# Sliding-window attention and a gated feed-forward layer on one core: the lead blocks' queries and keys loaded as fp32 by SyncE and ScalarE, and two lead blocks' scores also computed with the keys on the partitions

## The chip, the core and the metric

The kernel runs on one core of one Trainium2 chip. The metric is the device time of one execution in microseconds (us); less is better. A time is the median of several runs. A profile is one further execution, recorded by the hardware profiler.

## The reference

q, k and v are fp32 of 4 batches x 8 heads x 768 positions x 64. Each position attends to the first 4 positions (the sinks) and to the last 128 up to itself. The heads are put side by side, 3072 tokens of 512, and pass through a feed-forward layer with a hidden width of 2048. The output is fp32.

```python
scores = (1 / np.sqrt(D)) * np.matmul(q, k.transpose(0, 1, 3, 2))
keep = (pos[None, :] < n_sink) | ((rel >= 0) & (rel < window))   # 4 and 128
scores = np.where(keep, scores, -1e9)
a = np.exp(scores - scores.max(-1)); a = a / (a.sum(-1) + 1e-9)
x = (a @ v), heads side by side: (3072, 512)
h = x @ w_in; g = h / (1 + np.exp(-1.702 * h)); out = g @ w_out
```

## The kernel before, in words

**Tiling.** The 3072 tokens are 24 blocks of 128. A block's own keys and those of the block before it cover the window; the sinks are the batch's first 4 keys. Blocks 0, 6, 12 and 18 are the first of their batch. They have no block before them, and the 4 sinks are among their own keys. They run first (`ORD`) and are called the lead blocks here. Two blocks in the order of `ORD` make a group of 256 tokens for the feed-forward layer, so group 0 is blocks 0 and 6, group 1 is blocks 12 and 18, and there are 12 groups.

**A lead block's path.** Its queries and keys arrive as fp16 tiles `qkn` with tokens on the partitions. TensorE transposes them (`t_qk`, L408) into PSUM `tq`, and VectorE or ScalarE copies them to `qkT` (L282 to L288; the queries of a lead block are scaled on the way). TensorE first puts a mask into the PSUM tile `own` (`masks`, L455: identity times `bias0`) and adds the scores (`scores`, L463), queries on the partitions. VectorE takes each row's negated maximum (`mx`, L543). Half 0 of the heads goes through a subtraction on VectorE (`sub`, L600) and one exponential on ScalarE (L633). Half 1 is four exponentials on ScalarE with the maximum as bias (`exps`, L586). TensorE transposes the result so that keys are on the partitions (`t_a`, L696, PSUM `ta`), a copy makes `at`, TensorE multiplies by the values and a column of ones (`values`, L761, PSUM `av`), VectorE divides (`norm`, L776 and L777) into `xn`, TensorE transposes that (`t_x`, L790, PSUM `tx`), and a copy makes `xT`.

**The other 20 blocks** compute two score tiles (L488) and sink scores (L507), merge, take maxima and subtract on VectorE, take one exponential on ScalarE (L633), are transposed by DMA from SyncE's queue, and masked by two selections on GpSimd (L639, L645).

**The feed-forward layer.** `hT` (L825) is the first product; group 0 is split by block (16 matmuls of 128 columns per PSUM tile, tiles 0 to 3 for block 0 and 4 to 7 for block 6), the other groups use 8 matmuls of 256 columns. The gate is on ScalarE (L855), which loads a table whenever it changes between exponential and gate. `o` (L876) is the second product, 4 matmuls of 512 columns at a time. One tile `hT` and one such quarter of `o` both keep TensorE for about 0.87 us.

**Loads.** Only block 0's queries and keys come as fp32: `rawq` on SyncE's queue and `rawk` on ScalarE's (L237), each cast to fp16 on chip (L288). All other q, k, v and the weights are DMAs of GpSimd's queue, which cast on the way (L306, L315, L324, L333). Its order at the start is: q and k of 6, q and k of 18, k and q of 12, v of 0 and 18, q and k of 1, v of 6 and 12, three quarters of `w_in` (numbers 3, 1, 2), q and k of 2, `w_in` number 0.

**What sets the order.** The list `ORDER` names every operation by its number, with the engine that takes it, and each engine works through its own part of that list in order. An operation that waits holds up all that stand behind it on its engine. `FILL` puts matmuls on zeros (L905, into `misc`) ahead of given operations, 46 in all, every one of them before the first `hT`. `HOME` says for each PSUM tile which ring of banks it comes from.

Of the kernel before, what the change touches and what calls it, by code (L numbers as in the profile page):

```python
# [19 lines left out]
P = 128  # L20
D = 64
# [9 lines left out]
CFG = dict(  # L31
    tq=(0, 1, 2, 3, 4, 5, 6, 7),
# [10 lines left out]
    merge=4,  # L43
    pemask=(0, 1, 2, 3),
    f32=(0,),
# [8 lines left out]
RING = dict(qkn=4, qkt=4, e32=4, a16=4, at=4, atp=4, xn=2, xt=4, gt=3, osb=4, mm=3, own=2, pv=2, mi=1, th=2, ato=3, q0=4)  # L54
# [4 lines left out]
9V 4V 0S 17V 2V 15V 5G 13V 1S 22G 11V 19V 101S 18V 12V 7S 23G 6S 8S 28G 29G 20A 21A 3G 27G 108P 110P 109A 10V 113P  # L59
26G 16V 14V 130P 111V 114P 24G 32G 116V 131A 112A 132P 36G 133V 118A 115V 174P 37G 135P 117V 136P 175A 176P 138V  # L60
119A 154P 177V 25G 140A 120P 121A 137V 179P 31G 139V 180P 155A 152P 182V 35G 153V 141A 181V 33G 157P 184A 183V 142P
158P 34G 159V 122P 144P 185A 143A 40G 196P 123V 161V 126P 41G 145A 186P 160V 146P 198P 163A 148P 30G 127V 124P 187A
125V 46G 162A 188P 147V 164P 53G 149V 199A 166P 165V 150P 167V 189A 190P 168P 151V 128P 192P 169V 170P 129A 590P
171V 193V 582P 591A 197V 191V 172P 201P 47G 50G 586P 173A 194P 578P 583A 195V 587A 200P 579A 608P 49G 202V 610P 38G
55G 204V 203V 611A 609A 219P 221P 205V 588P 206V 589A 134A 580P 209V 208V 614P 39G 581A 105G 207V 222V 584P 42G 220V
576P 43G 585A 615A 612P 56G 577A 52G 613A 223P 604P 156A 225V 44G 226V 606P 45G 227V 616P 228V 224P 617A 607A 229V
232V 605A 230V 242P 618P 244P 231V 243V 592P 245V 626P 619A 210A 247P 246P 593P 249V 251V 248V 265P 267P 627P 250V
233A 620P 252V 266V 234S 254V 628P 268A 253V 621P 100S 255V 256A 211S 269P 622P 271V 257S 272V 594P 274V 288S 273V
629P 623P 624A 235G 270P 595P 630A 275V 104V 598P 596A 212G 599P 597S 276V 278V 631S 236P 277V 279A 238P 237V 600P
239V 59G 280S 213P 215P 51G 48G 214V 240P 601P 216V 241A 217P 602A 289P 61G 218V 290P 291V 642P 58G 292V 634P 71G  # L70
643A 294V 646P 293V 57G 295V 632P 68G 296V 647A 635A 297V 636P 62G 633A 306P 258G 640P 308V 309V 638P 641A 298V 310V
67G 73G 644P 311V 639A 637A 65G 648P 645A 654P 299A 64G 259P 655P 281G 307P 649P 312V 300S 313V 656P 314V 54G 261P
324S 315V 284P 260V 316A 650P 285V 262V 282P 657P 283V 301G 317S 178A 263P 286P 264V 651P 287V 603S 360S 664P 69G
652V 658A 662P 66G 665A 674P 60G 672P 70G 663A 675A 666P 78G 673A 325P 318G 660P 328V 327V 326P 304P 661A 667A 329V
668P 63G 330V 676P 669A 331V 74G 305V 670P 332V 302P 333V 671A 321P 303V 677P 322V 319P 682P 320V 334V 323S 342P
335A 344V 653S 345V 683P 678P 347V 343P 684P 346V 336S 348V 679P 350V 625S 351V 685P 349V 659S 352A 378P 692P 381V
686A 337G 353S 680V 379P 693A 696P 697A 380V 396S 690P 382V 80G 691A 383V 384V 688P 386V 76G 694P 385V 689A 102S
354G 387V 361P 695A 698P 364V 363V 700P 77G 699A 366V 340P 79G 701A 365V 338P 362P 388A 710P 339V 341V 355P 367V
711P 370V 368V 357P 356V 704P 389S 369V 702P 358V 371A 359S 414P 703A 705P 416V 372S 418V 712P 390G 417V 415P 706P
432S 419V 420V 713P 422V 83G 421V 707P 397P 82G 373G 708V 724P 400V 709S 399V 722P 423V 401V 714A 725A 393P 398P  # L80
402V 723A 391P 726P 392V 403V 394V 81G 716P 727A 85G 72G 718P 405V 404V 728P 719A 75G 374P 729A 717A 720P 86G 375V
106G 376P 721A 732P 406V 377V 424A 733P 395S 450P 738P 452V 407A 454V 451P 739P 453V 408S 730P 455V 456V 734P 457V
731A 715S 425S 458V 740P 433P 681S 746P 409G 436V 468S 435V 741P 747A 438V 735P 459V 742A 437V 92G 103S 758P 91G
434P 748P 759A 439V 426G 442V 736V 752P 749A 440V 756P 441V 753A 88G 744P 757A 95G 750P 745A 89G 412P 410P 413V 754P
107G 411V 429P 97G 755A 427P 430V 760P 751A 428V 443A 766P 431S 486P 767P 488V 460A 489V 444S 761P 490V 487P 762P
491V 461S 492V 768P 493V 743S 763P 494V 504S 445G 784P 764A 469P 785A 769P 472V 737S 462G 474V 495V 471V 782P 473V
772P 783A 470P 475V 87G 778P 773A 770V 98G 780P 446P 781A 84G 774P 447V 465P 775A 776P 466V 477V 779A 448P 777A 463P
476V 786P 464V 794P 449V 787A 478V 496A 467S 522P 788P 524V 525V 523P 789P 527V 479A 497S 795P 526V 528V 790P 530V
765S 529V 796P 480S 531V 532A 802P 94G 540S 498G 797P 803A 505P 798A 791P 507V 533S 96G 509V 800P 792A 481G 804P
499P 805A 810P 500V 90G 508V 814P 811A 510V 93G 501P 815A 506P 808P 511V 99G 801A 513V 484P 502V 812P 534G 482P 813A  # L90
806P 483V 809A 485V 822P 807A 514V 512V 503S 816P 515A 558P 687S 817P 793S 560V 559P 818P 562V 516S 823P 561V 563V
564V 819P 565V 567V 824P 566V 820V 568A 830P 517G 825P 831A 541P 834P 543V 826A 542P 535P 835A 827S 842P 536V 771S
544V 832P 569S 546V 833A 545V 821S 843A 547V 828P 799S 548V 836P 837A 550V 520P 829A 838P 521V 570G 549V 518P 839A
850P 551A 537P 538V 519V 844P 539S 851P 840P 552S 852P 841A 845P 573P 846P 574V 853P 553G 847P 854A 868P 855S 848A
856P 849S 869A 870P 857A 858P 871A 866P 862P 867A 859A 556P 554P 863A 557V 864P 571P 865A 860P 572V 555V 878P 861A
575S 872P 879P 873P 880P 874P 881P 886P 882V 875P 883S 887A 888P 876A 884P 877S 889A 894P 885A 890P 895A 896P 891A
892P 897A 898P 893A 906P 899A 900P 901P 907P 902P 912P 908P 903P 913P 904V 909P 914P 905S 910A 915P 911S 916A 917S
# [5 lines left out]
108:18 130:2 132:1 174:3 154:2 157:8 126:6 188:2 164:1 166:3  # L103
# [3 lines left out]
HOME = dict(x.split(":") for x in "0:pv 2:mm 5:own 7:own 8:mm 9:own 10:pv 12:pv 16:own 18:mm 19:pv 21:pv 22:mm 25:own 26:pv 27:mm 28:mm 29:pv 31:pv 32:own 35:pv 37:mm 40:own 41:pv 42:mm 43:mm 44:mm 46:mm 49:pv 50:pv 51:mm 52:own 53:own 54:own 55:pv 56:own 57:pv 59:mm 61:mm 62:own 63:own 64:own 65:pv 67:own 69:own 169:own 173:own 174:own 175:pv 180:pv 181:own 183:pv 185:own 189:pv 194:pv 197:pv 199:own 200:pv".split())  # L107
# [60 lines left out]
def kernel(  # L168
# [45 lines left out]
    bias0 = const.tile([P, P], BF16, name="bias0")  # L214
    bias1 = const.tile([P, 4], BF16, name="bias1")
# [16 lines left out]
    raw, o_raw = {}, {}  # L232
    for b in CFG["f32"]:
        for w, e in (("q", nc.sync), ("k", nc.scalar)):
            src = {"q": q, "k": k}[w][b // 6, :, b % 6 * P : b % 6 * P + P, :].rearrange("h s d -> s h d")
            raw[w, b] = const.tile([P, H, D], FP32, name=f"raw{w}{b}")
            o_raw[w, b] = hw(-3000, 0.4, lambda dst=raw[w, b], src=src, e=e: e.dma_start(dst, src), 0.7, late=1.15 if w == "q" else 0.3)  # L237
# [8 lines left out]
    )  # L246
    z_b = plan.add(DVE, -2002, 0.1, lambda: nc.vector.memset(bias0, 0.0))
# [18 lines left out]
    )  # L266
    z_k = plan.add(DVE, -90, 0.2, lambda: nc.vector.memset(ksb, 0.0))
# [12 lines left out]
    def copy(e, dst, src, factor=1.0):  # L280
        if e == DVE and factor != 1.0:
            nc.vector.tensor_scalar(out=dst, in0=src, scalar1=factor, scalar2=None, op0=ALU.mult)  # L282
        elif e == DVE:
            nc.vector.tensor_copy(out=dst, in_=src)  # L284
        elif factor != 1.0:
            nc.scalar.mul(out=dst, in_=src, mul=factor)
        else:
            nc.scalar.copy(out=dst, in_=src)  # L288
# [12 lines left out]
    def load_one(which, b, key, after, deps):  # L301
# [91 lines left out]
    for n, b in enumerate(ORD):  # L393
# [144 lines left out]
        mx = []  # L538
        for l in range(2):
# [6 lines left out]
                    deps=[packs[l]],  # L546
# [20 lines left out]
        subs = []  # L567
        a16 = Buf("a16", lambda n=n: a16s[n % RING["a16"]])
        bexp = []
        nbias, o_nb = small, top  # L570
        if nb and r > 0:
            nbias = const.tile([P, 2, 4], FP32, name=f"nb{b}")
            o_nb = plan.add(
                DVE, K0 - 38.75, 0.1,
                lambda nbias=nbias, small=small: nc.vector.tensor_scalar(
                    out=nbias, in0=small, scalar1=-scale, scalar2=None, op0=ALU.mult
                ),
                deps=[top, mx[0]],
            )
        factor = scale if r > 0 else 1.0  # L580
        for l in range(2):
            if l >= 2 - nb:

# [358 lines left out]
```

## Time and profile before

| | before |
|---|---|
| median of 3 runs | 227.57 us (227.36 to 228.15) |
| the profiled execution | 228.61 us |
| its span, first to last instruction | 226.9 us |
| mean granted TensorE clock | 1.000 |
| busy: TensorE, VectorE, ScalarE, GpSimd | 218.1, 138.7, 127.0, 115.3 us |
| first matmul of the feed-forward layer | 20.82 us |
| last eviction of an `o` tile starts | 223.76 us |
| matmuls of the feed-forward layer, L825 and L876 | 832 and 400 |

PE is TensorE's matmuls, PEld its weight loads, DVE VectorE, ACT ScalarE, POOL GpSimd, SP SyncE. A row of the time line gives the start and length of a run of like instructions, the engine, the line, the operation, the tiles written and read, and, in brackets, the idle time ahead of it with what ended it. The table of stretches gives for each stretch the busy time of each engine with the number of instructions, then the granted clock, the mean load of the DMA engines and what they moved in GB/s. A transfer that casts is counted with the bytes it writes.

### The profile page before, as it was taken

Reading aid. Unit: us, or ns where it says so; the run is one execution under the profiler, and the core shown is the slowest. Engines: PE = TensorE matmul, PEld = TensorE weight load, DVE = VectorE, ACT = ScalarE, POOL = GpSimd, SP = SyncE. Lnnn points to the kernel's source line nnn. Section 1 sums busy time; section 2 is a strip of 40 time slices with the busy share of each in tenths; the row PEclk is TensorE's granted clock in tenths of the full one; section 3 lists DMA queues with packets and bytes.
Section 4 is the critical chain, followed back from the end, with each engine's and each line's share of the span. In section 5 each row is a group of like instructions: output and inputs, shape, how many; then the busy total and the mean of one; then the engine's idle time right before and its main releaser. Section 6 shows DMA issues by size and latency. Waiting matters only on the chain.

```text
span 226.9 us, 5434 instructions
## 1 busy us (share of the span) xinstructions
PE 218.1 (96%) x2238; PEld 153.7 (68%) x2238; DVE 138.7 (61%) x332; ACT 127.0 (56%) x197; POOL 115.3 (51%) x127
## 2 busy tenths in 40 slices
PE   7889999999998999999999999999999999999994
PEld 4668997445774875775685685695695685775862
DVE  5799648876948288888976666668467582031001
ACT  3788675543663744767259347456656666540721
POOL 8995583029996970671980891570790321300000
PEclk9999999999999999999999999999999999999999
DMA  9999999999999999899997999998998175202202
GB/s 127 155 166 205 181 179 200 181 178 236 145 104 148 191 152 165 217 158 125 176 164 107 243 101 121 195 136 101 219 136 181 27 237 97 97 0 49 92 0 92
DMA packets 131992, 32.82 MB, mean 145 GB/s; under 512 B 124640, under 2 KB 129024, under 8 KB 131968
## 3 DMA queue, kind: packets, MB, share of 16 engines
q0 software_dynamic: 77024, 13.37, 78.1%
q1 hardware_dynamic: 53904, 18.85, 40.9%
q10 hardware_dynamic: 1040, 0.26, 0.5%
q8 instruction: 17, 0.28, 0.5%
q14 instruction: 7, 0.06, 0.1%
HBM read 27.36 MB, written 6.29 MB: 148 GB/s over the span
## 4 chain that ended last, share of the span: by engine, by line
PE 85%; DVE 7%; POOL 3%; ACT 2%; issue 1%; POOLq 0%; DVEq 0%
PE hT L825 35%; PE o L876 35%; PE own L488 3%; PE av L761 2%; PE av L765 2%; PE prv L488 2%; PE av L755 2%; DVE mx L562 2%; DVE mx L543 1%; POOL qkn L315 1%; PE tq L408 1%; DVE e L600 1%; POOL at L639 1%; ACT a L586 1%; PE tx L790 1%
## 5 line engine op out<-in xcount | busy, mean ns | idle before, releaser
L825 PE MATMUL hT<-xT,w_in 128*128 128x256 f16 (+1 forms) x832 | 91.9, 264 | 0.3 <-DVE osb L284 0.3
L876 PE MATMUL o<-w_out,gT 128*128 128x512 f16 (+1 forms) x400 | 90.5, 371 | 0.0
L855 ACT ACTIVATE gT<-hT 128x512 f16<-128x512 f32 x96 | 54.9, 597 | 49.9 <-PE hT L825 49.1
L825 PEld LDWEIGHTS <-w_in 128*128 128x128 f16 x832 | 74.0, 98 | 11.9 <-issue 0.7
L876 PEld LDWEIGHTS <-gT 128*128 128x128 f16 x400 | 36.5, 98 | 34.2 <-DVE own L531 0.4
L645 POOL TENSOR_SCALAR_AFFINE_SELECT atp<-at 128x1024 f16<-128x1024 f16 x20 | 22.1, 1104 | 71.2 <-DMA at<-a 54.7
L531 DVE COPY_PREDICATED own<-later,prv 128x512 f32<-128x512 uint16 x40 | 26.7, 692 | 25.4 <-PE prv L488 24.1
L633 ACT ACTIVATE a<-e 128x1056 f16<-128x1056 f32 (+1 forms) x24 | 23.8, 1007 | 18.2 <-issue 8.8
L543 DVE TENSOR_REDUCE mx<-own 128x4 f32<-128x512 f32 x48 | 31.9, 686 | 1.2 <-PE own L463 0.5
L600 DVE TENSOR_TENSOR e<-own,mx 128x512 f32<-128x512 f32 x44 | 28.9, 683 | 1.0
L639 POOL TENSOR_SCALAR_AFFINE_SELECT at<-at 128x1024 f16<-128x1024 f16 x20 | 22.3, 1113 | 1.4
L776 DVE RECIPROCAL rcp<-av 128x4 f32<-128x4 f32 x48 | 8.5, 176 | 23.4 <-PE av L765 23.2
L315 POOL DMA_DIRECT2D qkn<-in_k_dram x23 | 20.9, 911 | 2.8 <-DMA w_in<-in_moe_w_in_dram 2.4
L306 POOL DMA_DIRECT2D v<-in_v_dram x24 | 21.5, 907 | 0.8 <-DMA w_out<-in_moe_w_out_dram 0.8
L315 POOL DMA_DIRECT2D qkn<-in_q_dram x23 | 21.0, 913 | 1.8 <-DMA w_in<-in_moe_w_in_dram 1.7
L777 DVE TENSOR_TENSOR xn<-av,rcp 128x256 f16<-128x256 f32 x48 | 20.4, 424 | 1.7
L288 ACT COPY osb<-o 128x512 f32<-128x512 f32 (+1 forms) x17 | 9.2, 561 | 19.3 <-PE o L876 13.2
L761 PE MATMUL av<-v,at 128*128 128x65 f16 x192 | 16.7, 194 | 0.5 <-POOL at L639 0.4
L284 DVE COPY osb<-o 128x512 f32<-128x512 f32 x8 | 5.5, 688 | 18.5 <-PE o L876 18.1
L761 PEld LDWEIGHTS <-at 128*128 128x128 f16 x192 | 14.0, 98 | 3.1 <-POOL at L639 1.3
L765 PE MATMUL av<-v,atp 128*128 128x65 f16 x160 | 14.9, 194 | 0.0
L488 PEld LDWEIGHTS <-qkT 64*128 64x128 f16 x320 | 9.4, 94 | 7.0 <-issue 5.7
(59 smaller groups left out, 176.9 us busy)
## 6 DMA issues: line engine op xcount, KB each, us to landing
out_dram<-osb SPq DMA_DIRECT2D x23, 256.0 KB, 2.6
v<-in_v_dram POOLq DMA_DIRECT2D x24, 128.0 KB, 5.4
qkn<-in_q_dram POOLq DMA_DIRECT2D x23, 128.0 KB, 5.1
qkn<-in_k_dram POOLq DMA_DIRECT2D x23, 128.0 KB, 5.1
w_in<-in_moe_w_in_dram POOLq DMA_DIRECT2D x4, 512.0 KB, 10.1
w_out<-in_moe_w_out_dram POOLq DMA_DIRECT2D x4, 512.0 KB, 10.2
at<-a SPq DMA_TRANSPOSE x20, 3.5
rawk<-in_k_dram ACTq DMA_DIRECT2D x1, 256.0 KB, 4.5
```

The costliest lines, as they stand in the source:

```text
L306: return sw(key, 0.88, lambda: nc.gpsimd.dma_start(v65[:, b, :, 0:D], src), 1.0, deps=[z_1] + deps, after=after)
L315: key, 0.88, lambda: nc.gpsimd.dma_start(buf()[:, i, w], src), 0.9,
L531: nc.vector.copy_predicated(out=own[l](), mask=later.unsqueeze(1).to_broadcast((P, 4, P)), data=prv[l]())
L543: lambda l=l, own=own, small=small, r=r: nc.vector.tensor_reduce(out=small[:, l], in_=own[l](), axis=AX.X, op=ALU.max, negate=r == 0),
L600: nc.vector.tensor_tensor(out=e32()[:, 512 * l : 512 * l + 512].rearrange("p (j s) -> p j s", j=4), in0=own[l](), in1=small[:, l].unsqueez ...
L633: nc.scalar.activation(out=a16()[:, lo:hi], in_=e32()[:, lo:hi], func=AF.Exp, scale=factor)
L639: nc.gpsimd.affine_select(out=dst()[:, lo : lo + n], in_=at()[:, lo : lo + n], pattern=[[0, n], [1, P]], compare_op=ALU.is_ge, fill=0.0, b ...
L645: nc.gpsimd.affine_select(out=dst()[:, lo : lo + n], in_=at()[:, lo : lo + n], pattern=[[0, n], [-1, P]], compare_op=ALU.is_gt, fill=0.0, ...
L761: nc.tensor.matmul(av()[:, j], ato()[:, c], v65[:, b, h], start=(r == 0), stop=(r == 0))
L825: nc.tensor.matmul(ht()[:, n], w_in16[:, c, bass.ts(f, P)], xt[g]()[:, tok, c], start=(c == 0), stop=(c == 3))
L855: lambda fs=fs, cols=cols, gt=gt, ht=ht: nc.scalar.activation(out=gt()[:, fs[0] : fs[-1] + 1, cols], in_=ht(), func=AF.Gelu_apprx_sigmoid),
L876: nc.tensor.matmul(po(), gt()[:, F, bass.ts(t, P)], w_out16[:, F, cols], start=(F == 0), stop=(F == NF - 1))
```

## The change

1. **Loads.** Queries and keys of all four lead blocks come as fp32, four on SyncE's queue and four on ScalarE's, and are cast on chip, the cast now also possible on GpSimd. By the new order the casts are on ScalarE (q of 0, 6, 12), VectorE (k of 6, q of 18) and GpSimd (k of 0, 12, 18). ScalarE issues three loads ahead of its first table load and the fourth behind its first cast. GpSimd's queue of transfers then begins with v of 0 and 6, `w_in` 3, v of 12, `w_in` 0 and 1, v of 18, `w_in` 2, and q and k of 1; the casts stand between them.
2. **Scores with keys on partitions** for blocks 0 and 6 (`direct`). The scores are still computed with queries on the partitions and their maxima taken, but only for the maxima. VectorE splits the negated maximum into two bf16 parts (`nm`), TensorE transposes them (`tm`), a copy makes `nmt`. Two PSUM tiles `st` collect a transposed mask, the scores with operands exchanged and, through the 0/1 matrix `pick`, the maxima; two exponentials of 128 x 512 write `at` at once. The subtraction, the five exponentials, the transposes `t_a` and their copies are not made for these two blocks.
3. **Order.** `ORDER`, `FILL` (20 matmuls instead of 46) and `HOME` are new throughout. Ahead of the first `hT` there no longer stand: the transposes of block 1, the `t_a` of block 18, and the products `av` of blocks 12 and 18.

```diff
-    f32=(0,),
+    direct=(0, 1),
+    f32=(0, 6, 12, 18),
...
+            raw[w, b] = (
+                sb("osb", (P, d_model), FP32, f"raw{w}{b}") if n >= 2 else Buf("raw", lambda w=w, b=b: raws[w, b])
+            )
...
             return plan.add(
-                {DVE: 0.45, ACT: 0.6}, -95 + w, 0, lambda e: copy(e, buf()[:, i, w], raw[which, b]),
-                deps=[o_raw[which, b]], take=[buf],
+                {DVE: 0.45, ACT: 0.62, POOL: 0.75}, -95 + w, 0, 
+                lambda e: copy(e, buf()[:, i, w], raw[which, b]().rearrange("p (h d) -> p h d", h=H)),
+                deps=[o_raw[which, b]], take=[buf], give=[raw[which, b]],
             )
...
+            def shift(nm=nm, small=small):
+                nc.vector.tensor_copy(out=nm[:, 0], in_=small)
+                nc.vector.tensor_tensor(out=nm[:, 1], in0=small, in1=nm[:, 0], op=ALU.subtract)
...
+                lambda tpm=tpm, nm=nm: nc.tensor.transpose(tpm(), nm.rearrange("p a l j -> p (a l j)"), identb),
...
+            def masks_t(st=st):
+                for l in range(2):
+                    nc.tensor.matmul(
+                        st[l](), identb, bias0t.unsqueeze(1).to_broadcast((P, 4, P)), start=True, stop=False
+                    )
+            def scores_t(st=st, b=b):
...
+                        nc.tensor.matmul(
+                            st[l]()[:, j], qk_of(b)[rows, 4 + j], qk_of(b)[rows, j], start=False, stop=False
+                        )
...
+                def shift_t(l=l, st=st, nmt=nmt):
+                    for j in range(4):
+                        h = 4 * l + j
+                        nc.tensor.matmul(
+                            st[l]()[:, j], pick[:, h : h + 1].to_broadcast((16, P)), nmt, start=False, stop=j == 3
+                        )
...
+                        lambda l=l, st=st, at=at: nc.scalar.activation(
+                            out=at()[:, 4 * l : 4 * l + 4], in_=st[l](), func=AF.Exp
+                        ),
```

The three lists of the order are left out of this cut.

More of the change, by code (lines that the diff above doesn't have):

```diff
@@ L266 @@
     )
+    o_pick = None
+    if CFG["direct"]:
+        o_pick = plan.add(
+            DVE, -2000, 0.1,
+            lambda: nc.vector.tensor_tensor(out=pick, in0=identb[0:16, 0:8], in1=identb[0:16, 8:16], op=ALU.add),
+            deps=[o_identb],
+        )
     z_k = plan.add(DVE, -90, 0.2, lambda: nc.vector.memset(ksb, 0.0))
@@ L683 @@
+                subs.append(
+                    plan.add(
+                        DVE, K0 - 38.7, 0.6, sub, deps=[top if r > 0 else None, mx[l]], take=[e32], give=[own[l]]
+                    )
                 )
-            e_snk = None
             if r > 0:
-                e_snk = plan.add(
-                    ACT, K0 - 36, 0.15, lambda a16=a16, e32=e32, f=exp: f(a16, e32, 1024, 1056),
-                    deps=[subs[-1]] + zero, take=[a16], give=[e32], table="exp",
-                )
```

419 lines of the change are left out of this document (236 added, 183 removed).

## The prediction

> **What bounds the kernel now.** First the page's table of busy time, then the groups of instructions:
>
> ```profile
> PE 218.1 (96%) x2238; PEld 153.7 (68%) x2238; DVE 138.7 (61%) x332; ACT 127.0 (56%) x197; POOL 115.3 (51%) x127
> L825 PE MATMUL hT<-xT,w_in 128*128 128x256 f16 (+1 forms) x832 | 91.9, 264 | 0.3 <-DVE osb L284 0.3
> L876 PE MATMUL o<-w_out,gT 128*128 128x512 f16 (+1 forms) x400 | 90.5, 371 | 0.0
> ```
>
> TensorE is the bound, and the idle time ahead of its two big groups is 0.3 us in all. So from the first `hT` on, time is the work. What could be won lies before it. The time line of the start, and then of the end:
>
> ```profile
> 0.81 0.46 SPq L237 DMA_DIRECT2D rawq<-in_q_dram  x1
> 4.58 0.62 ACT L288 CAST qkn<-rawq 128x512 f16<-128x512 f32 x1 [1.98 <-DMA rawq<-in_q_dram]
> 5.30 0.62 ACT L288 CAST qkn<-rawk 128x512 f16<-128x512 f32 x1
> 7.04 0.42 DVE L284 COPY qkT<-tq 128x512 f16<-128x512 f16 x1 [1.16 <-ACT qkT L286]
> 7.52 0.40 PE L463 MATMUL own<-qkT 64*128 64x128 f16 x8 [0.27 <-DVE qkT L284]
> 7.96 0.69 DVE L543 TENSOR_REDUCE mx<-own 128x4 f32<-128x512 f32 x1 [0.49 <-PE own L463]
> ...
> 20.35 0.41 DVE L284 COPY xT<-tx 128x512 f16<-128x512 f16 x1
> 20.82 1.39 PE L825 MATMUL hT<-xT,w_in 128*128 128x128 f16 x22
> ...
> 223.76 0.37 ACT L288 COPY osb<-o 128x256 f32<-128x256 f32 x1 [0.46 <-PE o L876]
> ```
>
> The first `hT` starts at 20.82, once VectorE has copied the `xT` of block 6 at 20.35. VectorE works from 7.04 to there nearly without a break: the table of stretches gives it 12.63 us busy in the 14.32 from 6.50. So VectorE's queue sets the start. 46 of TensorE's matmuls there are fill and only look like work. The rest is an account in two parts: **T0**, the start of the first `hT`, and what TensorE does from T0 to 223.76, which is 202.94 us before. The end, 3.14 us of span behind 223.76, is built alike in both kernels and stays.
>
> **Part 1: T0 in the changed kernel.** I follow VectorE's new queue from the first item that waits for a load, the cast of k of block 6.
>
> Arrival of k6. `rawq` and `rawk` were issued at 0.81 and landed 3.7 and 4.5 us later. Now q6 and k6 stand right behind them in the same two queues. What the DMA engines moved while the two were under way:
>
> ```profile
> 2.00:2.50 0.50, 0.50 (x4) 0.38 (x3) 0.30 (x4) 0.50 (x1) 0.50 (x2) 1.00 0.89 205
> 2.50:3.00 0.50, 0.50 (x4) 0.34 (x3) 0.12 (x3) 0.10 (x1) 0.50 (x1) 1.00 0.73 167
> 3.00:3.50 0.50, 0.50 (x5) 0.35 (x3) 0.50 (x1) 0.00 (x0) 0.50 (x2) 1.00 1.27 287
> 3.50:4.00 0.50, 0.50 (x4) 0.38 (x3) 0.50 (x1) 0.00 (x0) 0.50 (x1) 1.00 1.35 280
> ```
>
> (The last column is GB/s.) Two pieces of 262 KB are 0.52 MB. Bounds for the next pair: 1.85 us at 284 GB/s, 3.1 us at 167. I take the faster, since two loads were moving in that row and a queue of loads is now behind them: k6 at 4.65 (mean of the two landings) + 1.85 = **6.5 us**.
>
> From there VectorE has, in order, by rows of before: cast of k6 0.45 (no row; bounds 0.20, the 128x128 cast L265, and 0.69, the fp32 128x512 subtraction; near the 0.42 of the 128x512 copy); queries of block 0 to `qkT` 0.42; wait for `own` 0.50 (7.46 to 7.96 above); two `mx` 1.37; the two `nm` operations 0.5 (0.19 as L615 and 0.34 as L562, both small); two copies to `ksb` 0.4 (0.197 each); `pick` 0.2; two `mx` of block 6 1.37; `nm` 0.5; cast of q18 0.45; copy `nmt` 0.2 (bounds 0.11, the smallest memset, and 0.42); two `mx` of block 12 1.37; subtraction 0.69; four `norm` 2.18 (0.545 from one to the next); `qkT` of block 18 0.42; three memsets 0.33; `xT` 0.41. That is 11.8. Before it was 8 `mx` 5.5, 4 subtractions 2.8, `qkT` 1.7, `at` 1.2, norms 2.2, `xT` 0.4 = 13.8. For handovers I add 0.5, about a third of the 1.7 that VectorE idled in that stretch before: **T0 = 6.5 + 11.8 + 0.5 = 18.8 us**, 2.0 earlier.
>
> What lies beside it. ScalarE: casts 3 x 0.62, four copies of 0.6, `nmt` 0.3, four exponentials 2.5 (0.63 each, L633, in place of the 1.14 + 0.63 per block), copy, then the exponentials of block 12 end near 18.2 and `xT` of block 0 near 19.4, while TensorE needs it for its second tile at 18.8 + 0.89 = 19.7. GpSimd's casts have no row; bounds 0.55 (half the 1.11 of the 128x1024 selection) and 1.17 (the 32x520 product L363). Cast of k0 from 5.3 to 6.1 stays ahead of VectorE's 6.5 to 7.4, so it is covered; uncovered, it would cost its excess one for one. The new work on TensorE per direct block, masks 0.43, scores 0.23, `tm` 0.06, maxima 8 x 0.055, against 0.44 for the `t_a`, fits where the 46 fills stood: nothing.
>
> Weights. GpSimd's queue issues `w_in` 3 behind the cast of k12, near 10; before at 12.28, landing 7.5 to 12.8 later. Its way is clearer: the first 12 transfers of that queue moved at 155 GB/s until 15, ahead of `w_in`; now two v do. At the 205 GB/s of the weights (2.55 us a piece) I estimate landings near 14.5, 18, 20.5 and 24 for numbers 3, 0, 1, 2. They are needed at 18.8, 19.7, 22.4 and 25.5: hidden by 1.5 us or more; with T0 below 17 they would be the next wait.
>
> **Part 2: from T0 to the end.** 202.94 stays, and what stood ahead of the first `hT` moves behind it: transposes of block 1 and `t_a` of 18, 16 x 0.055 = 0.88; `av` of 12 and 18, 16 x 0.03 = 0.48. Sum 204.3. Waits: the stall at 54.56, 0.38 us for GpSimd's selection of block 1, goes, since between the scores of block 1 and its `av` the new order gives 21 us and the gate tiles ahead of its exponential end as early as before. Other visible stalls (0.4 to 0.8 us each near 62, 70, 131 and 185) are redealt by the new order; zero on balance, bounds -2 and +2 (there were about 2.5 to lose). One new wait is in the open: the exponentials of block 18 stand ahead of the load of the gate's table, and the first gate then starts near 23.3, before at 22.62; by then four `hT` wait in PSUM. I cost it at nothing, since TensorE's fifth tile comes at 23.2 and the banks of block 18's transposes are free by then; uncovered 0.7.
>
> Sum: 18.8 + 204.3 - 0.4 = 222.7 against 223.76, **-1.1 us** of the profiled 228.61 (span 226.9). That run lies 1.04 above the median, so I take the difference: 227.57 - 1.1 = 226.5, own range 225.5 to 227.4 from the cast's bounds, handovers 0 to 1.2, and half of the redealt stalls. About 0.3% (0.7 us) can be told from no change.
>
> **The rivals.**
>
> *B, the loads come late; slower.* All waits on k6. At 167 GB/s two pairs need 6.3 us from 2.0, and the row of `rawk` has 0.7 between its last bytes and its cast: k6 at 9.0, T0 = 21.3, end 21.3 + 204.3 - 0.4 = 225.2, time 229.0. It decides for slower from a k6 at 8.3 on. For it: eight such pieces now stand where two stood. Against: 287 GB/s. The Trainium skill, "DMA: Bandwidth & Descriptors", section "Issuing engines are not separate DMA queues", says that loads issued from SyncE, ScalarE and GpSimd run on the same 16 DMA engines and that spreading them saves only issue time. The load column above 1 where both kinds ran agrees that they share. By that rule alone no pair would gain a rate, which is this rival.
>
> *C, the head start is eaten.* `hT` begins at 18.8 but TensorE waits: 0.7 for the first gate, and 0.4 to 0.8 in stalls of the new order (scores of blocks 3 and 4 come some 2.5 us later than before, their `av` 2.5 sooner). 226.5 + 1.1 = 227.6. For it: the table load ended at 22.62 before and cannot come earlier now.
>
> *D, more is won.* Casts at their lower bounds, k6 at 6.0, T0 18.0, and the new order loses 1.5 of the 2.5 stalls: 226.5 - 0.8 - 1.5 = 224.2.
>
> *E, TensorE goes slow in the gaps.* The first 18 fills took 4.02 us, 0.22 each, where 0.11 is the later rate; 26 of the fills are gone. If TensorE fell back to that rate before T0, the first 4 us of `hT` would take 2 more: 228.5. Against: no gap of TensorE's from 5.5 to 20.8 is longer than 0.91 us, and in the queues above I see none over 1. The Trainium skill, "TensorE: Matmul & The Clock Gate", section "What's actually happening", puts the fall at an idle window of about 3.4 us. By that rule E does not occur; the trace has no such gap to show it.
>
> That the change doesn't do what it says would need the loads to stay on GpSimd; the new queues show them moved.
>
> **Chances.** Forecast 0.48, B 0.13, C 0.20, D 0.14, E 0.05. Faster: 0.42 of the forecast, D, and 0.03 of C, 0.59. Within 0.3%: 0.06 of the forecast, 0.14 of C, 0.02 of B, 0.22. Slower: 0.11 of B, E, 0.03 of C, 0.19. Range 224.5 to 228.4: it holds the forecast, C, most of D and the near half of B and E.
>
> **What would show it.** VectorE's cast of k6 starting near 6.5; the first `hT` near 18.8, right behind VectorE's copy of `xT`; no wait of TensorE for `w_in`; first gate near 23.3; no gap at the selection of block 1. Wrong if k6 is cast after 8, if the first `hT` waits for `w_in` or ScalarE, or if TensorE's idle time behind T0 grows by over 1 us.

## The result, and the profile after

The changed kernel takes **231.07 us** (229.74 to 232.43, 4 runs) against 227.49 (227.36 to 228.15, 4 runs): ratio 1.0143, 95% interval 1.0100 to 1.0187. It is slower by 3.6 us; I had forecast 226.5, with 228.4 as the upper end. Its profiled execution took 231.13 us (span 229.4, granted clock 0.997). In the runs below, one execution each of e2, e6 and e8 (235.9, 234.9 and 235.2 us) fell into a slower state and is left out of their medians.

The page's busy time and two groups of instructions of the changed kernel:

```profile
PE 219.3 (96%) x2234; PEld 152.7 (67%) x2234; DVE 140.0 (61%) x344; ACT 125.4 (55%) x186; POOL 111.1 (48%) x124
...
L922 PE MATMUL hT<-xT,w_in 128*128 128x256 f16 (+1 forms) x832 | 93.3, 264 | 0.2 <-DMA xT<-xn 0.2
...
L858 PE MATMUL av<-v,at 128*128 128x65 f16 x192 | 16.8, 194 | 2.5 <-POOL at L736 2.5
```

And from the full lists of groups, the fills, changed and before; then before's wait of `av` (total, times, longest):

```profile
L1002 PE MATMUL misc<-fill 128*128 128x256 f16 x20 | 5.1, 383 | 1.1 <-DVE fill L286 1.1
...
L905 PE MATMUL misc<-fill 128*128 128x256 f16 x46 | 8.6, 330 | 1.1 <-DVE fill L261 1.1
...
PE av L761 <- POOL at L639: 0.4, 1, 0.4
```

TensorE is still the bound. The fills take 5.1 us instead of 8.6, yet TensorE is busy 1.2 us longer, and `av` waits 2.5 us for GpSimd's selections where it waited 0.4. The time line, from the cast of k6 to the last eviction:

```profile
7.88 0.72 DVE L317 CAST qkn<-rawk 128x512 f16<-128x512 f32 x1 [2.47 <-DMA rawk<-in_k_dram]
...
9.84 0.69 DVE L579 TENSOR_REDUCE mx<-own 128x4 f32<-128x512 f32 x1 [0.77 <-PE own L499]
...
11.18 0.82 DVE L616 CAST nm<-mx 128x8 bf16<-128x8 f32 x1
...
13.38 1.29 DVE L579 TENSOR_REDUCE mx<-own 128x4 f32<-128x512 f32 x2 [0.59 <-PE own L499]
...
21.03 0.42 DVE L317 COPY xT<-tx 128x512 f16<-128x512 f16 x1
...
21.60 1.95 PE L922 MATMUL hT<-xT,w_in 128*128 128x128 f16 x32
...
226.17 0.37 ACT L323 COPY osb<-o 128x256 f32<-128x256 f32 x1 [0.50 <-PE o L973]
```

k6 comes 1.4 us later than forecast, VectorE waits for `own`, and the first `hT` starts at 21.60 instead of 18.8, even behind the 20.82 of before.

**Where the time went.** No fill stands behind 30 us in any of the kernels. So TensorE's end is 30 plus the work left there plus its idle time behind it. One row of the table of stretches holds both (length of the stretch, then PE's busy time). For the changed kernel, to its last matmul:

```profile
30.00:226.14 196.14, 193.16 (x1919) 133.88 (x1916) 120.02 (x288) 106.02 (x147) 91.62 (x95) 1.00 1.15 141
```

And for a second profile of the kernel before (run e17 below, 227.53 us, at its median):

```profile
30.00:222.64 192.64, 191.39 (x1890) 132.22 (x1887) 114.78 (x272) 105.26 (x149) 92.40 (x95) 1.00 1.14 142
```

Work left: 193.16 against 191.39, 1.77 more. Idle: 196.14 - 193.16 = 2.98 against 1.25, 1.73 more. Together 3.5, the whole loss. One half was lost before 30 us, the other in waits behind it.

### The profile page after: what moved, and what is told of

Same layout as the page of the kernel before. It is cut to its first block, busy times and chain, and to the rows that moved or that the text cites. A ratio compares the mean times of both kernels' runs of the same rounds, so it can differ in the third digit from the quotient of the medians.

```text
span 229.4 us, 5445 instructions
## 1 busy us (share of the span) xinstructions
PE 219.3 (96%) x2234; PEld 152.7 (67%) x2234; DVE 140.0 (61%) x344; ACT 125.4 (55%) x186; POOL 111.1 (48%) x124
## 4 chain that ended last, share of the span: by engine, by line
PE 65%; DMA 15%; POOL 8%; issue 4%; ACT 3%; DVE 2%; SPq 0%; ACTq 0%; POOLq 0%
PE o L973 27%; PE hT L922 25%; DMA w_out<-in_moe_w_out_dram 5%; DMA qkT<-qkn 5%; DMA rawk<-in_k_dram 3%; POOL qkn L351 3%; POOL atp L742 2%; POOL at L736 2%; DMA xT<-xn 2%; PE av L858 2%; PE own L524 2%; PE av L862 2%; PE av L852 1%; PE prv L524 1%; PE tq L444 1%
## 5 line engine op out<-in xcount | busy, mean ns | idle before, releaser
L922 PE MATMUL hT<-xT,w_in 128*128 128x256 f16 (+1 forms) x832 | 93.3, 264 | 0.2 <-DMA xT<-xn 0.2
L730 ACT ACTIVATE a<-e 128x1056 f16<-128x1056 f32 (+1 forms) x22 | 22.7, 1041 | 12.1 <-issue 9.2
L699 DVE TENSOR_TENSOR e<-own,mx 128x512 f32<-128x512 f32 x42 | 27.8, 682 | 1.3 <-ACT gT L952 0.5
L323 ACT COPY osb<-o 128x512 f32<-128x512 f32 (+1 forms) x15 | 8.3, 554 | 23.4 <-PE o L973 20.2
L351 POOL DMA_DIRECT2D qkn<-in_q_dram x20 | 18.0, 901 | 5.6 <-DMA w_out<-in_moe_w_out_dram 4.6
L351 POOL DMA_DIRECT2D qkn<-in_k_dram x20 | 17.8, 895 | 2.9 <-DMA w_in<-in_moe_w_in_dram 2.4
L858 PE MATMUL av<-v,at 128*128 128x65 f16 x192 | 16.8, 194 | 2.5 <-POOL at L736 2.5
L317 DVE COPY osb<-o 128x512 f32<-128x512 f32 x10 | 6.9, 686 | 11.1 <-PE o L973 10.5
```

What stands on the lines that cost most here:

```text
L351: key, 0.88, lambda: nc.gpsimd.dma_start(buf()[:, i, w], src), 0.9,
L699: nc.vector.tensor_tensor(out=e32()[:, 512 * l : 512 * l + 512].rearrange("p (j s) -> p j s", j=4), in0=own[l](), in1=small[:, l].unsqueez ...
L730: nc.scalar.activation(out=a16()[:, lo:hi], in_=e32()[:, lo:hi], func=AF.Exp, scale=factor)
L858: nc.tensor.matmul(av()[:, j], ato()[:, c], v65[:, b, h], start=(r == 0), stop=(r == 0))
L922: nc.tensor.matmul(ht()[:, n], w_in16[:, c, bass.ts(f, P)], xt[g]()[:, tok, c], start=(c == 0), stop=(c == 3))
```

## The experiments

Theory after the result: (1) the start is late since 20 fills leave TensorE at about half its rate there and k6 lands late; (2) behind it a second bound, the way from GpSimd's loads by SyncE's DMA transposes to GpSimd's selections and `av`, takes what the start wins. Rival: the start alone; whatever it wins arrives at the end.

All medians in us; the kernel before beside them was at 227.5 to 227.9. Ratios to it with 95% intervals. "hT" is the start of the first `hT`, "left" and "idle" as above, all three from the one profiled run, which took the time given.

| run | median | ratio | profiled | hT | left | idle |
|---|---|---|---|---|---|---|
| before, first profile | 227.57 | | 228.61 | 20.82 | 191.81 | 1.92 |
| e17 before, second profile | 227.86 | 0.9992 [0.9955, 1.0028] | 227.53 | 20.78 | 191.39 | 1.25 |
| changed | 231.07 | 1.0143 [1.0100, 1.0187] | 231.13 | 21.60 | 193.16 | 2.98 |
| e1 changed, 35 fills | 229.20 | 1.0066 [1.0041, 1.0091] | 230.49 | 21.26 | 192.90 | 2.61 |
| e2 changed, one queue | 231.77 | 1.0208 [1.0151, 1.0264] | 231.56 | 22.83 | 194.30 | 2.23 |
| e3 before, 32 fills | 228.00 | 1.0014 [0.9980, 1.0048] | 228.17 | 21.89 | 192.36 | 0.93 |
| e4 changed, old loads | 232.15 | 1.0215 [1.0163, 1.0267] | 232.04 | 20.50 | 192.27 | 4.93 |
| e12 old loads, 35 fills | 229.96 | 1.0099 [1.0061, 1.0138] | 230.64 | 19.61 | 191.71 | 4.05 |
| e7 before + loads | 234.06 | 1.0281 [1.0252, 1.0309] | 234.46 | 25.26 | 196.78 | 2.66 |
| e11 before + scores | 234.13 | 1.0283 [1.0252, 1.0314] | 234.08 | 28.15 | 198.48 | 0.72 |
| e15 the same, interleaved | 230.41 | 1.0124 [1.0097, 1.0150] | 230.07 | 24.37 | 194.62 | 0.59 |
| e8 before, early prefetch | 230.44 | 1.0131 [1.0102, 1.0160] | 229.79 | 20.86 | 191.73 | 3.18 |
| e5 e1, late prefetch | 230.72 | 1.0128 [1.0102, 1.0154] | 231.03 | 19.94 | 191.58 | 4.45 |
| e6 e5, early k6 | 230.94 | 1.0155 [1.0134, 1.0176] | 230.70 | 21.60 | 193.21 | 2.50 |
| e9 e5, early v | 230.96 | 1.0153 [1.0126, 1.0181] | 230.50 | 20.44 | 192.28 | 3.20 |
| e10 e1, early v | 230.55 | 1.0119 [1.0086, 1.0151] | 230.73 | 21.13 | 192.62 | 3.12 |
| e13 e5, loads behind selections | 229.17 | 1.0073 [1.0051, 1.0095] | 229.31 | 20.92 | 192.51 | 1.80 |
| e14 e1, loads behind selections | 229.84 | 1.0096 [1.0068, 1.0124] | 229.81 | 21.16 | 192.56 | 2.26 |
| e16 e13, v5 back | 229.00 | 1.0027 [0.9996, 1.0057] | 230.19 | 21.90 | 193.48 | 1.68 |

A caution on the column hT: e1, e5, e13, e14 and e16 are the same program up to 40 us, and their profiles put the first `hT` at 21.26, 19.94, 20.92, 21.16 and 21.90. So in the new order one profile tells the start to some 2 us only. The three profiles with before's head (before, e17, e8) agree within 0.1.

### Fills and loads

**e1, e3.** Fills only.

```diff
 e1, changed:  -123:4 120:9 118:1 144:1 136:2 160:1 193:2
               +123:6 120:12 118:4 144:8 136:2 160:1 193:2
 e3, before:   -108:18
               +108:4
```

> The changed kernel with more fill matmuls ahead of the first blocks (43 instead of 20), so that TensorE has no gap of 0.9 us at 5.3 and 7.8. Clock theory (TensorE works at half rate until 12.8 because its early work is broken by gaps): four transposes in a row take 0.22 instead of 0.43 us from about 6 on, the first hT starts 1.0 to 1.5 us earlier (20.1 to 20.6) and the time falls by about as much, to 229.6 to 230.1. Load theory (everything waits for the keys of block 6): the keys still land at 7.9, the first hT moves by less than 0.3 us and the time stays at 231.

> The kernel before with 4 instead of 18 fill matmuls at its very start, nothing else. Clock theory: TensorE is idle from 2.2 to 5.5, its first transposes and masks take double time until about 9 to 12, the first hT starts 0.7 to 1.5 us after 20.82 and the time rises by as much. If the fills are no more than padding, first hT and time stay within 0.3 us.

15 more fills (35 instead of 20, not the 43 of the expectation) win 1.9 us in the median. TensorE's time line of the changed kernel in that stretch:

```profile
6.30 0.61 PE L444 MATMUL tq<-ident,qkn 128*128 128x128 f16 x4 [0.96 <-POOL qkn L319]
...
8.66 0.61 PE L444 MATMUL tq<-ident,qkn 128*128 128x128 f16 x4 [0.90 <-DVE qkn L317]
9.19 0.61 PE L499 MATMUL own<-qkT 64*128 64x128 f16 x8
...
10.31 1.06 PE L631 MATMUL st<-bias0t,identb 128*128 128x512 bf16 x2
```

And of e1:

```profile
7.36 0.39 PE L444 MATMUL tq<-ident,qkn 128*128 128x128 f16 x4
...
9.13 0.40 PE L499 MATMUL own<-qkT 64*128 64x128 f16 x8
...
10.09 0.59 PE L631 MATMUL st<-bias0t,identb 128*128 128x512 bf16 x2
```

Four transposes take 0.61 against 0.39, two masks 1.06 against 0.59: the changed kernel's TensorE runs at about half its rate until 12.8, e1's at full rate from 7. How that becomes 1.9 us is not shown: e1's one profile starts the first `hT` only 0.34 us sooner, less than such profiles scatter. In before, 14 fills fewer put the first `hT` back by 1.1 us, and the time hardly moves: its idle time falls to 0.93. (e1's profiled run took 1.3 us more than its median, so its idle time here is rather too high.)

**e2, e4, e12.** The loads.

```diff
 e2   -            for w, e in (("q", nc.sync), ("k", nc.scalar)):
      +            for w, e in (("q", nc.sync), ("k", nc.sync)):
 e4   -    f32=(0, 6, 12, 18),      # and q, k of 6, 12, 18 on GpSimd's queue behind bias0t
      +    f32=(0,),
 e12  = e4 with the fills of e1
```

> The changed kernel with all eight fp32 loads on SyncE's queue, none on ScalarE's. Load theory with two queues in each other's way (220 GB/s from 4 to 7.5, 288 once one of them is done): one queue moves at 288, the keys of block 6 land near 6.7 instead of 7.9, and the first hT starts about 1.2 us earlier. Load theory with the issue as limit (SyncE's issues took up to 2.3 us in the trace): twice as many issues on one engine, keys of block 6 no earlier, those of 18 later, time the same or up to 1 us more. Clock theory: TensorE as cold as before, first hT within 0.5 us of 21.6.

> The changed kernel with queries and keys of blocks 6, 12 and 18 on GpSimd's queue as before the change; scores with keys on partitions, the new order and its 20 fills stay. Load theory: queries and keys of 6 land near 6.8 as in the kernel before and VectorE's queue starts 1 us earlier; the first hT near 20.5 unless the later blocks' pieces now hold it up, time near 230. Clock theory: TensorE stays at half rate until about 12, first hT within 0.5 us of 21.6 and time near 231.

> The changed kernel's order and scores with the old loads of blocks 6, 12 and 18 (on GpSimd's queue, rounded by the DMA) as in the run with old loads (232.15 us), and with 35 fills instead of 20. Theory that cold TensorE and the backlog add: TensorE stays at full rate, 230.0 to 231.2, that is 1 to 2 us better, and the waits of av for GpSimd remain at 2 us or more since GpSimd again issues six loads more. If the clock were all that is wrong with old loads: 229.2 or less. If fills don't matter here: 231.7 to 232.5.

In one queue, k6 is there at the time that I had forecast:

```profile
6.45 0.65 DVE L317 CAST qkn<-rawk 128x512 f16<-128x512 f32 x1 [1.05 <-DMA rawk<-in_k_dram]
```

but k of block 18 is cast at 16.8, the first `hT` starts at 22.83, and the time is no better than the changed kernel's (the intervals overlap). So an early k6 alone would not have made the forecast. Four runs of the new order make a square: 20 fills 231.07 with the new loads and 232.15 with the old, 35 fills 229.20 and 229.96. The fills that were taken out cost about 2 us. The new loads seem to win about 1; each of the two differences is within the intervals. The old loads start the first `hT` sooner in their profiles, and yet end later: idle 4.05 to 4.93.

### One part alone in before's order

**e7.** The loads, with six casts put into before's order (its q and k of 6, 12, 18 no longer on GpSimd's queue). **e11, e15.** The scores of blocks 0 and 6. All three have before's 46 fills (44 in two of the expectations is a miscount).

```diff
 e11, block 0   -117V 118A 119A 120P 121A 122P 123V          (subtraction to at)
                +nm tm masks nmt scores shift exp shift exp   in one row behind mx
 e15            +nm masks | own of 6 | tm nmt scores | tq of 18 | shift exp | tq of 12 | shift exp
```

> The part of the change that concerns the loads, alone: before's order, its scores and its 44 fills, but q and k of blocks 6, 12 and 18 come as fp32 by SyncE and ScalarE and are rounded on chip by casts put into before's order (two each on VectorE, ScalarE and GpSimd). If the loads are what made the changed kernel late: 1 us or more over before (228.5 to 230), with waits of tq for casts of block 6 and the first feed-forward block later than 20.8. If the scores with keys on partitions, the fewer fills and the new order did it: the first feed-forward block at 20.3 to 21.0 and 227.0 to 228.0.

> The other part of the change alone: before's order, loads and 44 fills, with the scores of blocks 0 and 6 also with keys on partitions. What that part takes out of blocks 0 and 6 (subtractions, transposes of the exponentials and their copies) leaves before's order, and what it adds stands behind the two maxima of the same block. If this part is a gain that the loads and the order spoiled: the first feed-forward block 0.3 to 1.0 us earlier than 20.8 and 226.6 to 227.3. If it is even, as a chain that passes from VectorE to TensorE, ScalarE, TensorE and ScalarE: 227.2 to 228.0. If it is itself the loss: the first feed-forward block later than 21.3 and 228.3 or more.

> The scores with keys on partitions alone, in before's order, loads and fills as in the run of that part alone (234.1 us, first feed-forward block at 28.1), but with the chains of blocks 0 and 6 interleaved: the masks go ahead of the next block's scores, and the shift and the exponentials behind them. If it was my placement in a row that cost the 7 us at the start: the first feed-forward block at 22 to 25 and 229 to 232. If the part is a gain where TensorE finds other work between its steps: below 21 and below 228. If it is the chain itself: above 26 and above 233.

e7: q0's cast starts at 7.54 instead of 4.58, and the first `hT` at 25.26. The cast waits for ScalarE, not for its load. Before's order lets ScalarE issue all four of its loads ahead of its first table load:

```profile
0.80 5.41 ACTq L256 DMA_DIRECT2D rawk<-in_k_dram  x4
...
6.25 1.28 ACT L330 ACT_TABLE_LOAD   x1 [6.25 <-issue]
...
7.54 0.62 ACT L330 CAST qkn<-rawq 128x512 f16<-128x512 f32 x1
```

The changed order issues three there and ends the table load at 5.06, so e7 overstates what the loads cost. e11: TensorE waits for VectorE's maxima block by block:

```profile
PE tm L629 <- DVE nm L624: 3.2, 2, 1.9
```

e15 undoes 3.7 of the 6.5 us that e11 loses. Neither part is a gain in before's order as I placed it; both need an order built around them. My placements were not searched, so this doesn't show that no such order exists. The two also show how much of a late start reaches the end: the first `hT` is 7.4 and 3.6 us behind e17's, the last matmul 6.6 and 2.6 us. Most of it does; 0.8 and 1.0 us are made up, in part by less idle time (0.72 and 0.59 against 1.25).

### The second bound

**e8.** Before, with k8, q8, k9 issued by GpSimd ahead of its selections of blocks 2 and 1, as the changed order has them. **e5.** The reverse in e1.

```diff
 e8   +59G 58G 62G 235G ... 212G      (before: all three behind 235G and 212G)
 e5   -69G ... 72G ... 68G ... 226G 249G
      +226G ... 249G 69G 72G 68G
```

> The kernel before with one thing moved on GpSimd's queue: k8, q8 and k9 are issued ahead of the selections of blocks 2 and 1, as the changed kernel has them; nothing else changes. Theory of two bounds: GpSimd issues loads until about 40 instead of 37, the DMA transposes of blocks 1 and 2 land later, a wait of av for GpSimd's selection of 1 to 2 us appears between 50 and 60, and the time is 228.3 to 229.5. Rival, the head alone: within 0.3 us of before (227.3 to 227.9).

> The kernel of the run with 35 fills (229.2 us), with one thing moved on GpSimd's queue: the three prefetches k8, k9 and q8 are issued behind the selections of blocks 1 and 2, as they stand in the kernel before, no longer ahead of them. Theory of two bounds (the head of the kernel, and behind it the way from GpSimd's loads by the DMA transposes to the selections and av): the transposes of blocks 1 and 2 land within about 5 us instead of 9, the wait of av for GpSimd's selection (1.3 us in the profile with 35 fills, 2.5 in the changed kernel's) goes, and the time is 227.7 to 228.4. Rival, the head alone: the first feed-forward block starts as late as with 35 fills (about 21.3), the stall only moves to another tile, and the time stays at 228.9 to 229.5. If the prefetches are missed where they stood, new waits of tq or own for qkT between 55 and 75 would show it, and the time is above 229.5.

e8 is what the second bound foretells, with more loss: 2.9 us in the median for three loads of 0.9 us each in another place. TensorE's waits show where:

```profile
PE av L768 <- POOL at L646: 1.7, 2, 1.1
```

The issuing itself is not what holds the selections here. In e8 GpSimd has issued the three by 43.0 us and then stands idle until its next selection, block 2's. The same selection in e8 and in the kernel before:

```profile
51.13 1.09 POOL L652 TENSOR_SCALAR_AFFINE_SELECT atp<-at 128x1024 f16<-128x1024 f16 x1 [8.11 <-ACT osb L295]
...
49.62 1.09 POOL L645 TENSOR_SCALAR_AFFINE_SELECT atp<-at 128x1024 f16<-128x1024 f16 x1 [12.59 <-DMA at<-a]
```

What GpSimd waits for comes 1.5 us later, though block 2's transpose is issued at the same time (42.09 and 42.04). That this transpose lands later beside the three loads is likely but not shown; the view names a copy of ScalarE's as what ended e8's wait.

e5 is a miss for me. Its profile has the best start but one (19.94; left 191.58, level with before), and it is 1.5 us slower than e1. In its profile `av` waits longer:

```profile
PE av L865 <- POOL at L743: 3.9, 3, 1.6
```

**e6, e9, e10.** An earlier k6; and v of 0 and 6 and a quarter of `w_in` issued by GpSimd ahead of its first cast.

```diff
 e6        +for w, e in (("q", nc.sync if n < 2 else nc.scalar), ("k", nc.sync if n < 2 else nc.scalar)):
 e9, e10   -31G 11G 34G 35G 37G 45G
           +34G 35G 45G 31G 11G 37G
```

> As the kernel with late prefetches and 35 fills, but the fp32 loads of blocks 0 and 6 (q and k) are all issued by SyncE, and those of 12 and 18 all by ScalarE, so that the four that are needed first come in one queue. With all eight on SyncE k6's cast began at 6.45 instead of 7.9, so I expect 6.4 to 6.8 here, with q18 and k18 landed by 13. Theory of the head: the first feed-forward block starts 0.8 to 1.2 us earlier than in the kernel with late prefetches, and the time falls by as much, to 226.8 to 227.6. Rival, that what follows gives it back (two bounds, the second one not yet out of the way): the start moves by 0.8 to 1.2 us, the time by under 0.3. Rival, ScalarE: four issues there in a row push its casts and copies back, the start doesn't move.

> The kernel with 35 fills and late prefetches (its profile: first feed-forward block at 19.9, av waits 3.9 us for GpSimd's selections), with one thing moved: GpSimd issues the loads of v of blocks 0 and 6 and one quarter of w_in ahead of its first cast, in the 3.3 us in which it stands idle for k0. Theory that the prefetch through GpSimd's queue is the second bound (its backlog holds the DMA transposes up until about 50): everything behind in that queue is issued some 2.7 us earlier, the waits of av for the selections shrink to below 2 us, and the time falls by 1 to 2 us, to 228.7 to 229.7. Rival, order alone (each selection sits at a place found for one timing): no gain, 230.4 to 231.0. If the three loads take the DMA engines from the fp32 loads instead, k6's cast starts after 8.3 and the first feed-forward block moves back by as much.

> The kernel with 35 fills (229.2 us), with the same three loads (v of blocks 0 and 6, a quarter of w_in) ahead of GpSimd's first cast and the prefetches k8, k9, q8 left where the changed kernel has them. Theory that the backlog of GpSimd's queue is the second bound: the transposes of blocks 1 and 2 land 1 to 2 us earlier, the wait of av (1.3 us in its profile) goes, 228.0 to 228.7. Rival, the head alone: within 0.4 of 229.2, or later if k6 lands later.

All three miss: k6 came no sooner in e6 (7.92), and earlier loads of GpSimd's won nothing (e9) or lost 1.3 us (e10). So a backlog of GpSimd's first loads is not the second bound. But e1, e5, e6, e9, e10 and e12 agree in one thing: the first `hT` moves by 2.0 us among them, from 19.61 to 21.60, while left + idle stays at 195.5 to 196.0. In these profiles, what is won before 30 us comes back as idle time. (It is one profile each, and e1's run took 1.3 us more than e1's median; the medians, 229.20 to 230.96, don't follow the start either.)

**e13, e14, e16.** In e5 two of the three waits of `av` follow on loads in GpSimd's queue. GpSimd's time line in e5:

```profile
68.48 0.89 POOL L348 DMA_DIRECT2D v<-in_v_dram  x1
69.36 1.12 POOL L749 TENSOR_SCALAR_AFFINE_SELECT atp<-at 128x1024 f16<-128x1024 f16 x1
...
77.67 1.09 POOL L749 TENSOR_SCALAR_AFFINE_SELECT atp<-at 128x1024 f16<-128x1024 f16 x1 [6.03 <-DMA at<-a]
...
81.63 1.78 POOL L358 DMA_DIRECT2D qkn<-in_k_dram  x2
83.37 1.14 POOL L749 TENSOR_SCALAR_AFFINE_SELECT atp<-at 128x1024 f16<-128x1024 f16 x1
```

The selections of blocks 4 and 7 start without a pause behind loads, while GpSimd stands idle for 6 us between. So e13 moves v10, q13, v5 and v9, k16:

```diff
 e13, e14  -64G 58G 61G 77G 76G 80G 272G 78G 67G 295G 315G 83G 73G 90G 81G 332G
           +58G 61G 77G 272G 78G 67G 295G 76G 80G 64G 315G 83G 81G 332G 73G 90G
 e16       as e13, with 64G (v5) and 67G (v7) exchanged
```

> The kernel with 35 fills and late prefetches (230.7 us; av waits for selections at 52.8 by 0.9, at 71.7 by 1.4, at 85.7 by 1.6 us), with five loads moved in GpSimd's queue: v10, q13 and v5 from ahead of the selections of blocks 3 and 4 to behind those of block 4, where GpSimd then stands idle for 6 us; v9 and k16 from ahead of the selections of block 7 to behind them. Theory that GpSimd's queue is the second bound (loads at 0.9 us each ahead of the selections that av waits for): the selections of block 4 start 2 us earlier and those of block 7 1.5, the waits at 71.7 and 85.7 fall below 0.5 us each, and the time is 228.0 to 229.5. Rival, the DMA transposes' landing is what the selections wait for: no change, 230.4 to 231.0, with GpSimd idle ahead of the same selections.

> The kernel with 35 fills (229.2 us), with the same five loads moved behind the same selections. Its profile shows waits of av at 53.4 and 57.2 only (1.3 us), none at 71 or 85, so by the theory of GpSimd's queue little is to be had there: 228.8 to 229.4. If it falls below 228.5, these loads cost it more than its waits show; above 229.8, the loads are missed where they stood.

> The kernel with five loads behind the selections (229.17 us), with v of block 5 back ahead of the selections of block 4 and v of block 7 behind them in its place: in that kernel's profile av of block 5 waited 0.7 us for its values, and block 7's are not needed before 80. Theory of GpSimd's queue: this wait goes and none takes its place, 228.3 to 229.0, still above before, since TensorE has some 0.7 us more to do after 30 us than in the kernel before. Rival: the wait moves to the next selection, 229.0 to 229.5. If it reached 227.9 or less, idle time behind 30 us would be all that the change cost.

GpSimd's time line in e13:

```profile
66.47 1.12 POOL L749 TENSOR_SCALAR_AFFINE_SELECT atp<-at 128x1024 f16<-128x1024 f16 x1
...
76.28 1.09 POOL L749 TENSOR_SCALAR_AFFINE_SELECT atp<-at 128x1024 f16<-128x1024 f16 x1 [4.90 <-DMA at<-a]
...
80.69 1.09 POOL L749 TENSOR_SCALAR_AFFINE_SELECT atp<-at 128x1024 f16<-128x1024 f16 x1 [0.42 <-PE av L869]
```

Both selections come 2.7 to 2.9 us sooner, `av`'s wait for GpSimd falls from 3.9 to 0.5 us, and the time by 1.55. The same move in e1, which had no such waits, wins nothing (e14). e16 takes away e13's new wait for v5; its interval reaches before's time, though the medians stand 229.00 to 227.85. Where `av` waits little, the end does follow the start: from e13's profile to e16's (waits for GpSimd 0.5 and 1.0 us) the first `hT` is 0.98 later and the last matmul 0.85.

**e17.** Before, unchanged, for a second profile.

> The kernel before, unchanged, profiled a second time. Its first profile was of a run of 228.61 us, 1.04 above the median, with 1.9 us of TensorE idle behind 30 us, 1.6 of them between 50 and 90. If those waits vary from run to run, a run near 227.6 shows less than 1.2 us there; if the head varies, its first feed-forward matmul starts earlier than 20.82.

The first `hT` hardly moves (20.78). TensorE's idle time between 50 and 90 is 0.55 us instead of 1.56: the 1.04 us by which the first profile stood above the median are waits there that vary from run to run.

## Why the prediction was wrong

**What bounds it.** Wrong: "from the first `hT` on, time is the work. What could be won lies before it." With 0.3 us of waits at the two big groups it looked so; I take it that those groups stay busy because the blocks' `at` come just in time. The profiles of e5 and e12 start the first `hT` 0.8 to 1.2 us before e17 does and end 3.1 to 3.4 us later; e15 starts it 3.6 us after and loses 2.6. A late start costs most of itself, an early one won nothing here.

**T0 = 18.8, the step that failed first; 21.60.** Two terms were mis-sized, half each. *k6 at 6.5*: its cast starts at 7.88, 1.4 late. I took the faster bound, 284 GB/s, since "two loads were moving in that row". Behind 4.0 us the DMA engines moved less, with eight loads on their way:

```profile
3.50:4.00 0.50, 0.50 (x4) 0.38 (x3) 0.39 (x1) 0.22 (x1) 0.00 (x0) 1.00 1.28 286
4.00:5.00 1.00, 1.00 (x7) 0.60 (x4) 1.00 (x1) 1.00 (x1) 0.00 (x0) 1.00 1.35 224
...
6.00:7.00 1.00, 0.70 (x6) 0.65 (x7) 0.00 (x0) 0.00 (x0) 1.00 (x3) 1.00 1.36 212
```

The rate is not the whole of it. In e2, with all eight loads in one queue, the engines moved 224 GB/s from 4.0 to 6.5, and k6 is cast at 6.45. In e6, with the same first four in the same order on SyncE's queue and the last four on ScalarE's, they moved 288 in that stretch, and k6 is cast at 7.92. The faster stretch has the later k6. So there the loads of the second queue, which move at the same time, delay it; my sum gave q6 and k6 the engines to themselves.

*The 12.3 from there*: 13.72. The casts are 0.72 and 0.64 instead of 0.45 each (+0.5), the first `nm` 0.82 + 0.17 instead of 0.5 (+0.5), and VectorE's waits 0.77 + 0.59 + 0.62 instead of 0.5 and 0.5 of handovers (+1.0), less 0.6 on smaller items. (My lists add lengths that overlap a little: the 13.8 for before stands against 12.63 busy in its trace.) With TensorE at full rate, e5 needs 12.29, the forecast, but e1, e13 and e14 need 13.3, so in three of these four profiles the rate explains only 0.4 of the 1.4.

Why the casts are longer is not shown. In seven profiles (changed, e1, e2, e5, e13, e14, e16) GpSimd ends an issue of loads while VectorE casts k6; the cast takes 0.65 to 0.79 and ends 0.24 to 0.26 behind that issue. In e6, e9 and e10, where no issue ends beside it, it takes 0.43. It looks as if the issue holds VectorE up; no run was made for it.

Rival B came nearest (slower, T0 21.3), but by luck of the sum: it needed k6 at 9.0, and k6 came at 7.88. Of my signs of being wrong, k6 after 8 did not show; TensorE's idle time did grow by over 1 us.

**"fits where the 46 fills stood: nothing."** Wrong, 1.9 us by e1, 2.2 by e4 and e12. The fills were not idle time to be used up: with 15 more of them TensorE came to its full rate at 7 instead of 12.8. That is rival E's cause in another place: I priced it in the first 4 us of `hT`, and it fell on the chain of the scores. I gave it 0.05 since there was no gap over 1 us. The changed kernel's longest there is 0.96.

**Weights and first gate.** Weights: right, no wait for `w_in`. The gate starts at 25.86 instead of 23.3, and no wait of TensorE for it shows.

**Part 2.** From T0 to the end 204.57 (226.17 - 21.60) against 203.9 forecast. The moved work, 1.36, and a start 0.8 later would make 2.2; 1.77 more is left at 30 us. The waits, "zero on balance, bounds -2 and +2", are the second step that failed, and the other half of the loss (1.73): the stall for GpSimd's selection of block 1 didn't go but grew from 0.38 to 2.1 us with that of block 2. e8 shows that the place of three loads in GpSimd's queue is enough for that, e13 that the queue is what the later ones hang on. But e5, with the three loads put back, was no faster, so the loads' place is not all of it. That is rival C (a head start eaten) by another way than the gate. It would probably have eaten most of a start at 18.8 too: e12 at 19.61 ends no sooner than e1.

**The offset.** I carried the 1.04 us between profile and median over to the changed kernel. Its profiled run is at its median, and e17's profile lacks the waits that make up the 1.04.

**What stays open.** The transposes of block 1 are issued at 41 to 44 us, and the selections behind them start between 48.8 and 51.7 in all kernels of the new order but two (e2, e4: 53.6, 52.0). What holds those landings there was not settled: less in GpSimd's queue ahead of them (e5, e9) changed it by 1 us at most. Nor is it shown why the start of the new order varies by 2 us between profiles, or how much of the work left in e13 and e16 is the two blocks' extra matmuls.

## What to carry to other kernels

An operation that stands ready just in time gives no wait to see: before counting on a head start, move the start alone, earlier or later (e3), and see whether the end follows; profile a kernel more than once before reading a start from it. Fills are part of the schedule where TensorE waits often; take them out only where its matmuls' spacing shows full rate without them. Where one in-order queue issues loads and also does work that is waited for, count each load ahead of it (0.9 us here) as part of that wait, and put loads into the queue's idle time (e13).

## What the runs showed of the hardware

TensorE can fall back to half rate within a stretch of short gaps. In e4 it ran at full rate at 5.8; from the table of stretches (PEclk is the third number from the end):

```profile
6.00:8.00 2.00, 0.84 (x14) 0.61 (x11) 0.56 (x3) 0.59 (x1) 2.00 (x3) 1.00 2.15 137
8.00:9.00 1.00, 0.66 (x14) 0.48 (x12) 0.42 (x1) 0.59 (x1) 1.00 (x3) 0.74 2.25 143
9.00:10.00 1.00, 1.00 (x6) 0.57 (x5) 0.96 (x4) 0.49 (x1) 1.00 (x2) 0.50 2.27 144
```

TensorE was busy 0.84 of 2.0 us, with no gap over 1.16, and then had 0.50 of its clock until past 11. The Trainium skill, "TensorE: Matmul & The Clock Gate", section "What's actually happening", puts the fall at an idle window of about 3.4 us; here it came right behind a stretch that was busy less than half the time, without any such gap. In the changed kernel's profile the same column reads 1.00 in all stretches up to 13 us while the spacing shows about half rate until 12.8: a TensorE that has not yet come up to rate shows in the matmuls' spacing, not in that column.

Issuing loads held the issuing engines up in the changed kernel: ScalarE's first three took 2.94 us from 0.80, SyncE's second pair 2.26 us at 3.13; in e7 ScalarE's four took 5.41 us.
